# A threshold-attention and maxout-FFN kernel on one core: the same instructions in another written order, with other PSUM slots and another choice of masked score halves

## The chip, the cores and the metric

The kernel runs on one core of a Trainium2 chip. The core has a matrix engine (PE, called TensorE), a vector engine (DVE, VectorE), an activation engine (ACT, ScalarE), a general engine (POOL, GpSimd) and a queue that issues transfers (SP, SyncE). Each engine takes its own instructions in the order in which the program lists them, and semaphores hold an instruction back until what it needs is there. The metric is the device time of one execution in microseconds (us); smaller is better. Three runs of the kernel before took 442.86, 443.29 and 444.62 us, so the median is 443.29 us.

## The reference, cut to what matters

Eight batches of eight heads, 576 positions, head size 64. Scores that lie more than tau = 0.02 below their row's maximum are dropped, the rest go through a softmax. The result is the input of a feed-forward part with three first matrices, of whose products the elementwise maximum is taken.

```python
scores = scale * np.matmul(q, k.transpose(0, 1, 3, 2))
thresh = np.max(scores, axis=-1, keepdims=True) - tau
scores = np.where(scores >= thresh, scores, -1000000000.0)
scores = scores - np.max(scores, axis=-1, keepdims=True)
attn = np.exp(scores)
attn = attn / (np.sum(attn, axis=-1, keepdims=True) + 1e-09)
attn_out = np.matmul(attn, v)
...
x = attn_out.transpose(0, 2, 1, 3).reshape(B * S, H * D)
h = np.maximum(np.maximum(x @ w1, x @ w2), x @ w3)
out = h @ w_out
```

## The kernel before, in words

The attention is cut into 16 groups of four heads (a batch has two), and a group into nine chunks of 128 query rows and two halves each: 288 *score halves* of 128 x 576 in all. One letter of a long text, ORDER, issues one piece of work. The program at its end walks through this text, and every engine is wrapped so that its instructions stay in that order (class `_Ordered`). The letters that this document uses:

- `S` and a digit: the score matmuls of the next half, into one of four PSUM slots, the digit; a slot is two banks. `T` and a digit: transposes of queries and keys for a group (for the first group both into two slots, the digit's and the one two further on, with two small `warm` matmuls into slot 3 after the first of them). `O`: attention times values, `F` and `B`: the two halves of a feed-forward piece (tile `ph` for the hidden layer, `po` for the output), `N`: a piece of output rows.
- `m`: DVE reads a score half from PSUM, writes a copy `z` to SBUF and its row extreme `nm`. `s`: a tiny DVE instruction makes the threshold `th`. `e`: ACT makes exponents or clips at the threshold. `n`: ACT makes the exponents and their sum (an ACTIVATE and an ACTIVATION_READ_ACCUMULATOR). `k`: DVE drops what lies under the threshold and sums (SCALAR_TENSOR_TENSOR). `r`: DVE takes the reciprocal of the sums. `p`: POOL normalizes into `P`. `t`: SP issues the transposing transfer of `P` into `ptq`.
- `a`, `c`: ACT and DVE evacuate transposed queries `qt` and keys `kt`; `q`: POOL (for the first group DVE too) makes `qs`, a copy with the two 64-row halves swapped. `x`, `w`, `h`, `v`, `u`: evacuations of `O`, `F` and output pieces on ACT (`x`, `h`, `u`) and DVE (`w`, `v`).
- `l`, `g`: SP issues loads of inputs and of weights; `z`, `y`: POOL casts weights and values; `o`, `i`, `d`: stores.

A second text, MASKED, has a digit for each score half. It decides between two ways to the same numerators. For 0 and 2 (not masked) the half costs `m` on DVE and `e` and `n` on ACT; 0 also costs `s` on DVE. For 1 and 3 (masked) it costs `m` and `k` on DVE and `e` on ACT. With 2 and 3 (direct) `e` reads the scores from PSUM instead of `z`, and holds the slot until then.

Attention and feed-forward are interleaved: the first hidden-layer piece stands after the 54th score half, the last score half after some 140 of the 180 `F` pieces. The four PSUM slots are shared by all PE pieces, so a piece cannot start before the last reader of the piece that had its slot.

Of the kernel before, what the change touches and what calls it, by code (L numbers as in the profile page):

```python
# [21 lines left out]
FLAT = 2.0 ** -100  # L22

MASKED = """
320220312002220000101010000320210002020210010010301000000010100000001101
001001011010101100001000000000110000101010001111011000100000100010000000
110001001110100100010000001000111000000100011011101000011000010000010000
010101000111000100100000000101000000011110001110101000000000101000011121
"""


# [22 lines left out]
peBmF2pnvS0npS1rsmBnptmF3eT0ssvBatS1khF2qlemS0BerrpmT1epF3svtF0nsqcBeS2pvnBtpmeS1oyrS3mhpS2nmptF1nsmS0pleBrm
pF3nvS2teT0sslmF1eBkaBnsrqvS2hS0qmeF3ptmS1nBpsmnF2prevS0F1ptessmBpeBsvtF3hkS0lnBrmpleS1vT2peO0mnlscnT3lrwS1p
aF2mepS0treBpmF3nvyT1qnBcS0hpF2srempS1teS3mqBnkS0ptnO1smemteF3rvxlT0BskaS2evqS1npmS0tnysS3meF2smpermqeT0S1sc
pnBrmtepkyS0uS3muyS1epmS2lnF0pmoermpelS3skpO2elklnkO1elswnrmByxektpS1usrS3umS2peF0mpeS1mBynpsmtF3hS2srknpBtm
eS1F0pveF2sntmBnT3rvpS1atBpmeS0yrS3shmqtS1essF2mpeF0kqnF3smBetBrpvnlBprevS1lphS2lmnS0pmF3eptrS1mnBpmnF0ptsS2
veBosmeF1svT3nBtrecpS2hF0pmtnF3skBeT1srvS2paBtemqF0lnvS1pS2emBqermS3pnF1smT2eBchS3lskeT2O0lkakeqO2mtnsqlvS3x
wpS1nsrF2mpeF0rmpBestS3pevByemS1hS2tmpT3nF0rsmpnF1cBpeBtveT3S2rnvpS0astmpS1nmyS3eyF2smqnrstmepS1lnqS0mBelpsm  # L60
elkT1uS0ceS3lmeO1rknpiO0ewpumtnF1kelkxS2lkeS3sBrmepntpmF0uorS2rpuBnmyS3hsF1tmepT2lBkapS0essvS3eN2pmtnrmpF0ek
pS1jtBrnmF3lpnvS2opS1smeS0mBetS2mhS1ersmpF3tnF0kpBemF2sBrsevpBkF1qhtvS3nS2srpnrmBpeS0mF3pnmF2yteBvpeT0svqF1e
tBsscF3hkBnT2vS0aBemlqS2nvpF0nT1rmpBesS3cphF2rsmtpeS1rS0pnmS3teqBmF1epsvS0ntpsBmelT2ymO3evntrspF1welS0kaBnmS
3qS2hmpS0nrsF1mqeS3smpF2eBtrsmpnBvnpS0sS3epmS1etrvO0pelmekS2yxtmS3eF0mnpmnyT1yssrkS2npBemtpeclS3urS2pmuS1nsm
T0tO3akoeqO2elwpnlkT0eyrF3cximeqlS0snpBmeptskS1uF0mnBsurkpF1hrS2eBpmteS0pvF3lnS2prmeBpstF1mnF0peslvBkS2hS3rm
peBtrF1epsmT2npvBtaF3kpS0nsvBtemqS2ohS1rymnpF0sS3metpBemT2nF1rscpF3evBtqnBsvpS2hsrS0pemS1npmF2temT3S0assBnmF
3tnvS1S0ermpBemS2peF1svS0nmBerS3mpthS2kF0pnF1smeBrempO3nsvpteskF2qnBwBnrvtpT0eF3srscqS1hBepmT0S2vaS1smnqT3S0
mtnqF2secT1yBparmS3eqvS1eS0mpeF2mpempT3nS1ctqnS0smBermtnpS3kepS1muF0usrskpeS3meS2tpmeS1oBknmemnO3kuurO2kyxeO
1wetpsnkpS0xS2meF1rmnS3pBrsptmS0hF2pemS3perF1smBptnsS0vpeF3ktN2emeskBjF0rnvptBersS2pohBpF1evpF3nmBtnBkO0hsvt
eS2wrS1nrpmF3npsmS2eBpsmF1npvS0eytS2rsymBnpF3veipS0mBS1mhtF2nrsF3mpeBstpS1evF0emBeBvtS1hsF2nmS3nF0rsmpF1ekBp  # L70
nBvBesvO2hO3rkxpntS1rweS0pmF3nmpS2F1spremBpteBvpS0eS2vtS3mF1metkeF0mnnBrkpekBukurO1upoO2xpO1wprN3xptuF2jpF1h
F0tvF3vF1hF2vtF0vF1hF2vF0ovF1hF3vF2ivF1hF0vF2vF3hF0vO2vO3wF1xF0uF2hF3voF0vF2hF3vF1vF0hF2vF1vF0hF2vF1vF3hF2vF
0vF1hF2vF0vF2uF1ouN2ofjdi
"""


# [753 lines left out]
```

## Time and profile before

| what | value |
|---|---|
| median of three runs | 443.29 us (442.86 to 444.62) |
| the profiled execution | 443.79 us, of which the span from first to last instruction is 442.0 us |
| instructions | 14289 |
| busy: PE, DVE, ACT, POOL | 420.4, 398.2, 402.3, 319.5 us |
| weight loads of PE (PEld) | 318.1 us |
| mean granted TensorE clock | 0.987 of full speed |

The busy times are unions of an engine's instructions, so instructions that overlap in the engine's pipeline count once. The end of a matmul is modelled, and a busy PE is not one that works at its peak. A row that ends in `<-DVE z` tells that the engine stood idle before the instruction until DVE had written a tile `z`. Nearly all instructions carry line L93, that of the wrapper that keeps the order, so pieces are told apart by tile names.

### The profile page before, as it was taken

The numbers are of one execution on the slowest core, as the hardware profiler recorded it, in microseconds if no ns is written. First come the engines' busy times: TensorE is split into PE (matmuls) and PEld (weight loads), VectorE is DVE, ScalarE is ACT, GpSimd is POOL, SyncE is SP. The second block draws the span as 40 slices with busy tenths as digits, with TensorE's granted clock in tenths as the row PEclk, the third lists the DMA queues.
The fourth block names the chain that finished last, engine by engine and source line by source line (L and its number), as shares of the span: only waits on it lengthen the run. The fifth ranks groups of instructions, "written<-read, shape, count | busy, mean of one in ns | idle before, by whom it ended". The sixth has DMA issues, their size and how long they took to land.

```text
span 442.0 us, 14289 instructions
## 1 busy us (share of the span) xinstructions
PE 420.4 (95%) x5188; PEld 318.1 (72%) x5190; DVE 398.2 (90%) x1252; ACT 402.3 (91%) x828; POOL 319.5 (72%) x420
## 2 busy tenths in 40 slices
PE   8686879999999999999999999999999999999996
PEld 7453447787687777787788777787688786786873
DVE  3888899999999999999999998999999999899542
ACT  3999999999999999999999999999999999998421
POOL 1799999999889589866987676777777776555400
PEclk9998899999999999999999999999999999999999
DMA  6998999999999999999999999999999747987702
GB/s 190 280 294 175 258 197 240 274 222 270 232 241 250 222 204 228 220 200 236 200 227 224 215 173 244 209 200 198 178 252 197 124 82 129 185 132 110 188 25 85
DMA packets 213959, 88.50 MB, mean 200 GB/s; under 512 B 189184, under 2 KB 202240, under 8 KB 213888
## 3 DMA queue, kind: packets, MB, share of 16 engines
q1 hardware_dynamic: 213360, 86.96, 99.1%
q8 instruction: 41, 0.67, 0.6%
q10 hardware_dynamic: 528, 0.62, 0.5%
q14 instruction: 30, 0.25, 0.2%
HBM read 35.65 MB, written 9.44 MB: 102 GB/s over the span
## 4 chain that ended last, share of the span: by engine, by line
PE 84%; DVE 6%; ACT 5%; issue 2%; POOL 1%; DVEq 0%; POOLq 0%; ACTq 0%
PE ph L93 31%; PE sc L93 28%; PE po L93 10%; PE o L93 9%; ACT z L93 5%; DVE z L93 4%; PE tp L93 4%; PE warm L93 1%; POOL P L93 1%; DVE kt L93 1%; ACT qt L93 1%; DVE hm L93 0%; DVE stage L93 0%; DVE hT L93 0%; DVE th L93 0%
## 5 line engine op out<-in xcount | busy, mean ns | idle before, releaser
L93 POOL TENSOR_SCALAR P<-z,rs 128x576 bf16<-128x576 f32 x250 | 202.4, 821 | 61.5 <-DVE rs L93 23.3
L93 DVE TENSOR_SCALAR_CACHE_REDUCE z<-sc 128x576 f32<-128x576 f32 x250 | 184.1, 750 | 11.4 <-PE sc L93 5.2
L93 PE MATMUL sc<-kt,qs 64*128 64x256 f32 (+2 forms) x640 | 181.7, 419 | 8.2 <-DVE z L93 4.5
L93 PE MATMUL sc<-kt,qt 64*128 64x320 f32 (+2 forms) x640 | 182.2, 429 | 6.2 <-ACT z L93 2.7
L93 PE MATMUL ph<-xt,w 64*128 64x288 bf16 (+2 forms) x2160 | 171.3, 283 | 0.2
L93 PEld LDWEIGHTS <-w 64*128 64x128 bf16 (+1 forms) x2160 | 127.8, 94 | 32.2 <-issue 4.3
L93 ACT ACTIVATE z<-z,th 128x576 f32<-128x576 f32 x157 | 118.2, 770 | 1.7 <-DVE th L93 1.1
L93 ACT ACTIVATE z<-z 128x576 f32<-128x576 f32 x170 | 114.8, 678 | 0.3
L93 PEld LDWEIGHTS sc<-kt,qs 64*128 64x128 f32 (+1 forms) x640 | 93.4, 180 | 25.4 <-DVE z L93 9.5
L93 PEld LDWEIGHTS sc<-kt,qt 64*128 64x128 f32 (+1 forms) x640 | 93.2, 180 | 17.1 <-DVE z L93 5.2
L93 DVE SCALAR_TENSOR_TENSOR z<-z 128x576 f32<-128x576 f32 x80 | 67.2, 850 | 0.8 <-ACT z L93 0.8
L93 POOL COPY qs<-qt 64x640 f32<-64x640 f32 (+3 forms) x66 | 46.6, 705 | 23.0 <-ACT qt L93 19.7
L93 ACT ACTIVATE z<-z,nm 128x576 f32<-128x576 f32 x76 | 57.7, 767 | 1.1 <-DVE z L93 1.1
L93 PE MATMUL po<-wo,hT 64*128 64x512 bf16 (+3 forms) x454 | 53.1, 355 | 0.4 <-issue 0.2
L93 DVE TENSOR_TENSOR hm<-ph,hm 128x576 bf16<-128x576 f32 (+2 forms) x54 | 37.0, 685 | 10.9 <-PE ph L93 10.0
L93 ACT ACTIVATE hm<-ph 128x576 bf16<-128x576 f32 (+2 forms) x54 | 31.8, 589 | 13.0 <-PE ph L93 12.8
L93 PEld LDWEIGHTS <-hT 64*128 64x128 bf16 (+2 forms) x456 | 28.4, 95 | 18.7 <-issue 2.2
L93 DVE TENSOR_TENSOR hT<-ph,hm 128x576 bf16<-128x576 f32 (+2 forms) x54 | 37.0, 686 | 2.5 <-PE ph L93 0.7
L93 PE MATMUL o<-ptq,vb 128*64 128x512 bf16 (+2 forms) x544 | 38.7, 282 | 0.5 <-DVE z L93 0.5
L93 ACT ACTIVATION_READ_ACCUMULATOR z<-z 128x1 f32 x170 | 33.4, 196 | 0.0
L93 PEld LDWEIGHTS <-vb 128*64 128x64 bf16 x544 | 22.7, 111 | 13.9 <-issue 5.8
L93 POOL TENSOR_SCALAR P<-stage,rs 128x576 bf16<-128x576 f32 x38 | 29.5, 781 | 3.6 <-DVE rs L93 2.2
(44 smaller groups left out, 422.1 us busy)
## 6 DMA issues: line engine op xcount, KB each, us to landing
vm<-in_v_dram SPq DMA_DIRECT2D x32, 256.0 KB, 4.8
qm<-in_q_dram SPq DMA_DIRECT2D x15, 512.0 KB, 4.9
km<-in_k_dram SPq DMA_DIRECT2D x15, 512.0 KB, 5.6
out_dram<-ob SPq DMA_DIRECT2D x14, 512.0 KB, 3.9
stage<-in_moe_w_dram SPq DMA_DIRECT2D x9, 512.0 KB, 5.4
ptq<-P SPq DMA_TRANSPOSE x144, 4.5
vr<-in_v_dram SPq DMA_DIRECT2D x16, 128.0 KB, 3.7
stage<-in_moe_w_out_dram SPq DMA_DIRECT2D x3, 512.0 KB, 5.4
```

The lines of the kernel that those rows point to most:

```text
L93: ins = fn(*a, **kw)
```

## The change

Only the two tables change. The functions, the shapes, the pools and the numbers above them (36 warm matmuls, four slots, nine `z` buffers) stay.

```diff
 MASKED = """
-320220312002220000101010000320210002020210010010301000000010100000001101
+220202110002002100110000100020020312000112012010100000000010100000001100
...
 ORDER = """
-lllllllllT1lcaqqlT2S3agcqqmlS2S0elmlkeT1lmnS2lscS0aelrmS3plmeqmlqnS2zeslS1mT3nlpS0maygecreqekpS2nmnpT3meyskS
+lllllllllT0laqqlcT1aS2lcqqgmS0S3lemS1lmnT2lmeS3lsaS0mnqlqemT3lyerclcapsnS1lS2eqmlS3qemznmS2perS1mnpsmnpT3ske
...
```

Counted over the whole texts, the new MASKED has 187, 84, 14 and 3 of the digits 0, 1, 2 and 3, where the old one has 185, 86, 13 and 4. So 87 halves are masked instead of 90. ORDER keeps the kinds and numbers of all pieces apart from what follows from that: 201 `n` instead of 198, 87 `k` instead of 90, 187 `s` instead of 185. PE's large pieces keep nearly the same sequence; the digits of the slots, and the places of the short DVE, ACT, POOL and SP instructions between them, differ almost everywhere.

Counted in the written order, the ACT instructions ahead of the 60th score half are 114 in both (56 `e`, 41 `n`, 13 evacuations of transposes, 2 `x`, 2 `h`), ahead of the 72nd 138 in both, ahead of the 96th 190 before and 193 now, ahead of the 144th 293 and 295, ahead of the 216th 448 and 451.

Three places follow as rows of one engine's program. The first is DVE at the very start, where the first group's keys and queries come out of PSUM. Before:

```order
L93 MEMSET vr_102 64x64 x2
L93 COPY kt<-tp 128x320
L93 COPY qs<-qt 64x320
L93 COPY qs<-qt 64x256
L93 TENSOR_SCALAR z,nm<-sc 128x576 x2
L93 SCALAR_TENSOR_TENSOR z,sm<-z 128x576
```

and now:

```order
L93 MEMSET vr_102 64x64 x2
L93 COPY qs<-qt 64x320
L93 COPY kt<-tp 128x320
L93 COPY qs<-qt 64x256
L93 TENSOR_SCALAR z,nm<-sc 128x576 x4
L93 TENSOR_SCALAR th<-nm 128x1
```

The copy of the keys moves behind the copy of the swapped queries, and the first masked half's SCALAR_TENSOR_TENSOR is gone from here. At the same place the first transposes move from slot 1 (with 3) to slot 0 (with 2), and the second from slot 2 (with 0) to slot 1 (with 3). The two `warm` matmuls between them use slot 3 as before.

The second place is ACT over the same first microseconds, up to its first clipped half (`z<-z,th`). Before:

```order
L93 ACTIVATE qt<-tp 128x320
L93 ACTIVATE qt<-tp 128x256
L93 ACTIVATE kt<-tp 128x256
L93 ACTIVATE z<-sc,nm 128x576 x2
L93 ACTIVATE z,sm<-z 128x576
L93 ACTIVATE qt<-tp 128x320
L93 ACTIVATE z<-z,th 128x576
```

and now:

```order
L93 ACTIVATE qt<-tp 128x320
L93 ACTIVATE qt<-tp 128x256
L93 ACTIVATE kt<-tp 128x256
L93 ACTIVATE z<-sc,nm 128x576
L93 ACTIVATE z,sm<-z 128x576
L93 ACTIVATE z<-sc,nm 128x576
L93 ACTIVATE qt<-tp 128x320
L93 ACTIVATE z,sm<-z 128x576
L93 ACTIVATE z<-z,th 128x576
```

The first half is no longer masked, so its exponents and sum (`z,sm<-z`) follow on ACT at once, ahead of the second half's first instruction.

The third place is SP's queue around the loads of the third batch's first group (tiles `qm_870` and `km_872` before, `qm_901` and `km_903` now). Before:

```order
L93 DMA_TRANSPOSE ptq_736<-P_955 128x9x128
L93 DMA k8_873<-in_k_dram 128x4x64
L93 DMA stage_1036<-in_moe_w3_dram 128x4x256
L93 DMA qm_870<-in_q_dram 128x2x512
L93 DMA stage_1053<-in_moe_w1_dram 128x4x256
L93 DMA_TRANSPOSE ptq_1072<-P_999 128x9x128
L93 DMA km_872<-in_k_dram 128x2x512
```

and now:

```order
L93 DMA_TRANSPOSE ptq_749<-P_931 128x9x128
L93 DMA stage_1035<-in_moe_w3_dram 128x4x256
L93 DMA_TRANSPOSE ptq_1054<-P_1012 128x9x128
L93 DMA k8_904<-in_k_dram 128x4x64
L93 DMA qm_901<-in_q_dram 128x2x512
L93 DMA km_903<-in_k_dram 128x2x512
```

One transposing transfer of the next group now stands ahead of the load of the queries, and the load of the keys comes right behind it instead of two rows later.

More of the change, by code (lines that the diff above doesn't have):

```diff
@@ L24 @@
 MASKED = """
-320220312002220000101010000320210002020210010010301000000010100000001101
-001001011010101100001000000000110000101010001111011000100000100010000000
-110001001110100100010000001000111000000100011011101000011000010000010000
-010101000111000100100000000101000000011110001110101000000000101000011121
+220202110002002100110000100020020312000112012010100000000010100000001100
+001000111010000101100000000000110001100000011110110200100000100010000000
+110001101110100100010000001001100100000100101111102300000100100000001000
+001000110100100001000000000100100001011110100011011100002100001000001013
 """
@@ L71 @@
[L71 to L73 removed]
+lllllllllT0laqqlcT1aS2lcqqgmS0S3lemS1lmnT2lmeS3lsaS0mnqlqemT3lyerclcapsnS1lS2eqmlS3qemznmS2perS1mnpsmnpT3ske
+ytS1erkpT2agmnT3pclesqS2aqetS0meqlrnspmS1eqsT2nmpS3tnrcS0zlemS2eprmS3npmtS0npsgS1sermpS2emyS3eptmT0eplmS1ayl
+meS0kynS2tssT3snkynkercperlT3pmnpmntqremS0lasprgeT3pmeS2psstnplnS0mzecesqrmS3etqkeS2gpnmS1npsmtnS0prmleS3pmS
@@ new lines @@
+2npsmnS0yrsmetperS2epmO1eqtnkplemnzswT2teS3rplS1empnmS3tpnssrS1klepS0mapermtS2epmT1S3nmqtnkO2qemncpS3txrskT1
+peS2rmeS0ptmegpamS2npS1ertsmpnlkzS2elmS3eS0mpnlO1srkepsmnO2tyeprgwnpmT1xS3cpeS0sszmF2eS1meBqkF0ngqT3shrsmBay
+S2tvpnF3rpemS1BpemF0pnsvT2BnyctS1esrlsT2mphS3lezS1maF0myntpT2sS3ngrcqF1eBmpnS2svpBnrmS3peS0tmeyF2zmnF3lBsvep
+S0rhkBptesF2mgeS1zvF0nsmBpteBsrgvpnF1kS3phS2semBnqmF0S3evqF2ntrmBpelS1spvBnlmS3qhF0rsmepS1tnBpsmS3ezvS2eS1rm
+pF0etsyO3mnlkngpO2eswetkBxrmpT3nF2rvpaS1BnqmS0hspS3meF2prS1smntBzesmF3ezvT0tBeclT1yS2pnvS0apsmtS3eyrmlS1epS2
@@ new lines @@
+mepF0mnqsmnS3tkBnkeF1restpkumeS2prtBumlperkpS0ustS2umS3pesmS1eqtT0mO2nlpceqsrmO3ntywelkS0pxlS1meF3prnS2smBye
+myF0thpskS1oeBpF2nlvF3nlrmBpeBkpS1hstsvS0eF3lrmpnF2mBepBsveF1nT0vBtarkS3lhqS2smleF0prF1mnBysntBveS2plvnS0pom
+F3nyS1pmeBsysmF0thT2rrlpeS1clF3epsmBnqT2svBaS1evqS2nmF0pS3nmqBtnmT2pS1hrcpS3esmS0petF2melS1rmpBnF3skpetF0sve
+BlBmnF2vhtF1esrBkpnS0vtT3npBmS2arvpS0ermO3eqtsmepT1swntpS0cF2epesmtnS3kT1nS0mtBessrkpameS3preS1mS0uqmuS3mpnS
+1tsmS2pnoS0rempS3lempO1lnkqlemO2lnymeO0srkpetkeF3swxykxpT2BercnprtS1uyS2upmF0termqS3eBymN2lhsskpelkS0eF3ertm
@@ new lines @@
+S1pjBlmeS0plvF2npS1mnyF3tpmnBsopT0nvBaS1kF2ieqrssmS0hlpBmelT1qF3snrvF0epcBlepS2vBnpsmtS1nS3rmphS2mnpF1smeS0B
+snmF3tevS2T0mF1atBrsekpBevS0thS2pmF3nymS1qeBrsmnpS0tvF2eplF1rmnpBskeBptF3hsvS0eBrsstpmnS1lvT2qeO0mpnlscnT3wS
+1etF2srramS0lnqBmlF3eqvT1nBcpS0thF2pemS1perS3mpBnmS0ptesO1smpnkteF3yvxT0BraktyS2esS1vpeS0mpnS3meqF2mnyrmpnT0
+S1lceBqmeptrskS0pulS3muS1epmS2teF0rmplnskpeS1mtO3eklekO2esrmpesBknpwxS1kutS2urmopS3nF0myeS1mBetpsmF2hlS3rkep
+BlmnF0S1prnsvT3tepBmF2apsssvS1eBtqmeS0qrS3hmtS1epsmF2lnpF0mleF3koBnBrvpeBstyvS1phsS2nmF3emS0nrS1tpmBnprS2smn
@@ new lines @@
+F0pveF1pBsremT3ptevBpS2chF0tnmF3ekBT1nvS2aBsmlnF0qvS1eS2rtrespmS3eBmqF1hmpT2nBcpS3ekpT2O0sasvterlmpO2ekqntwS
+3xklpS1eF2ssmnF0yrBnmyS3evBptemS1plhS2ssmT3eyF0rcpeF1mBpntT3vnByS2ravpS0nmtpS3nsmS1eF2srmpektepS3slmnS0Bmeqn
+mT1ktuS3urS0lcpeO2rlmpelmpeO3klpelweF1kqnsxS0rkepS2tmS3eBymemepS0kuF3quT2smeBtrF1kphoS0aBmnpS3tsN2rnvplnmpS1
+erkpF0tjsF3mnBpsseBvS2ihrS1pmelS0mqeF3S2mnytBpmnoS1rF0eprsvF2ntpmBeBvqF1htskpS3esS0rmetS2pnmF3pBnmF0pesvT2te
+BcF1nsBrvpntBskphT2F3erS0vlapBmnF1qvS2etpBmT0hS3rscpnF2lmS1qesS0sempBemS3yF1nvtS0nmBnT2ssrmpO3etspveF0wnS1rk
@@ new lines @@
+BpaS3tmhS2elqsF1mlS0qnmS3ermpBF2espsmS0npvBeS3tmeS1rvpO0ntmnsmS2yxS3empF0eskyerT1mpeS2cBtnypsmelkS3ulS2muS1e
+smT0O3nsrplnpO2awetmeF3rkpxseT0S1ycntS2meF0poBrnsmpnkpF1ukBurS2shBqemF3oepvS0lS2nsmqF1emBptBnvF0hrrS2speS3mp
+F1emBpntT2vepF3BssaktS0nvlBemS2hS1rsmptF0nS3mpeBmtnT2F1svnF3cetBBsrnvpS2hsrqS0meS1pmeT3F2sprmaS0npBmeF3ptsvn
+S1qS0mnBtqmeS2yF1prevS0epssBmnS3qmS2htpmF0nlF1keBsmBertvO3pnvepF0serwpT2nBcpF3hktS1eBsrsmpnT0S2vtpaS1remqT3S
+0nmyF2qectT1BpasmS3epvS1nS0mqnF2rmpemtpT3eS1keqS0smBercntpS1mupS3emF0ukessS1rmtpnBmopkS2uskS1eO3rukekO0yxeO3
@@ L74 @@
+ynwtprmopS0xmpS2emF3peS1mteBrsmpS0nF2pmhtS1nkBS3evF0nstmN2erkpeF1mBjpsBevS2hskF0eF3rkpteBmF1nBpveBkO2hsrvpeS
+0rtwS1pnmF2npmS3eBympF1ntrvS0epBmpS2rF3svtpeS0mnpS1sBmiF2smhF0ntkBBervpS1etF3smpnF2BervpS1hsBpnmF0tevS3F1nmB
+etrBkpO2vhO3nspS1xrwepS0mpF3smS2etF1snmBeBstvnS2S0veS3meF1snkeF2rmpnmpeBnkBerrptukpuO3rN1xpuO0jpuO3wptF1xpF2
+hF0tvF1vF3hF0vtF1vF2hF0viF1vF2ohF0voF1vF3hF2vF1vF3hF2vO1vO0wF2xF3F1huF0vF3vF2ohF1vF3vF2hF0vF1vF3hF0vF2vF3hF1
+vF2vF0hF1vF2vF0uF1ouN0ofjdi
 """
```

29 lines of the change are left out of this document (removed).

## Prediction

> **What bounds the kernel now.** The page's first line has the busy time of each engine; three are close together.
>
> ```profile
> PE 420.4 (95%) x5188; PEld 318.1 (72%) x5190; DVE 398.2 (90%) x1252; ACT 402.3 (91%) x828; POOL 319.5 (72%) x420
> ```
>
> Which of them sets the pace differs by stretch, so the next view is the table of busy times by stretch. After the stretch and its length come the busy time of PE, PEld, DVE, ACT and POOL, with the number of instructions, then the granted TensorE clock.
>
> ```profile
> core 0: us, PE busy (x) PEld busy (x) DVE busy (x) ACT busy (x) POOL busy (x), PEclk, DMA share, GB/s
> 0.00:20.00 20.00, 14.53 (x132) 10.93 (x132) 11.67 (x38) 12.05 (x25) 8.53 (x18) 1.00 0.90 243
> 20.00:40.00 20.00, 15.97 (x138) 10.63 (x138) 17.47 (x57) 20.00 (x43) 19.05 (x27) 0.91 1.16 252
> 40.00:60.00 20.00, 14.80 (x114) 9.15 (x114) 17.67 (x60) 19.92 (x45) 19.17 (x25) 0.83 1.03 204
> 60.00:80.00 20.00, 18.07 (x226) 13.44 (x224) 19.67 (x66) 19.99 (x42) 18.20 (x23) 1.00 1.12 244
> 80.00:100.00 20.00, 19.99 (x264) 15.39 (x262) 19.54 (x63) 19.97 (x44) 19.12 (x27) 1.00 1.17 240
> 100.00:400.00 300.00, 299.29 (x3942) 231.85 (x3940) 289.79 (x919) 292.59 (x597) 225.66 (x294) 1.00 1.06 202
> 400.00:420.00 20.00, 20.00 (x239) 15.06 (x232) 14.41 (x40) 12.50 (x28) 9.79 (x12) 1.00 0.71 158
> 420.00:442.00 22.00, 17.73 (x152) 11.63 (x151) 7.93 (x16) 5.25 (x12) 0.00 (x0) 0.97 0.16 55
> ```
>
> There are two regimes. From 20 to 100 us ACT is busy for 79.88 of 80 us, while PE idles. From 100 to 400 us PE is busy for 299.29 of 300 us, and ACT has 7.41 us left over. So the time is a sum of four: until ACT runs without a gap, ACT's work up to the point where PE has enough queued to run without a gap, PE's remaining work, and the tail after PE's last matmul. The next view, PE's waits, agrees: first from 0 to 80 us, then all there are from 80 to 420 us.
>
> ```profile
> PE sc L93 <- DVE z L93: 6.6, 11, 1.2
> PE sc L93 <- ACT z L93: 3.7, 5, 1.3
> PE sc L93 <- DVE th L93: 1.5, 1, 1.5
> ...
> PE sc L93 <- DVE z L93: 0.2, 1, 0.2
> ```
>
> The scores wait for their slot's reader, but nearly all of it happens early, while ACT sets the pace. In the chain that ended last PE has most of the span:
>
> ```profile
> PE 84%; DVE 6%; ACT 5%; issue 2%; POOL 1%; DVEq 0%; POOLq 0%; ACTq 0%
> ```
>
> The profiled execution took 443.79 us, 1.8 us more than its span and 0.50 us over the median of 443.29 us. I work out a difference to the span and put it on the median.
>
> **The change part by part.**
>
> *Three halves go from masked to not masked.* Prices, from the costliest groups and the groups by line:
>
> ```profile
> L93 ACT ACTIVATE z<-z 128x576 f32<-128x576 f32 x170 | 114.8, 678 | 0.3
> L93 DVE SCALAR_TENSOR_TENSOR z<-z 128x576 f32<-128x576 f32 x80 | 67.2, 850 | 0.8 <-ACT z L93 0.8
> ...
> L93 ACT ACTIVATION_READ_ACCUMULATOR z<-z 128x1 f32 x170 | 33.4, 196 | 0.0
> L93 DVE TENSOR_SCALAR th<-nm 128x1 f32<-128x1 f32 x185 | 25.4, 144 | 0.5
> L93 DVE DVE_READ_ACCUMULATOR z<-z 128x1 f32 x80 | 6.3, 79 | 0.0
> ```
>
> ACT gets three more pairs of 678 + 196 ns, 2.6 us by durations. Neighbours overlap: in the next fence (the timeline of ACT's start, start and length in us) the pairs that begin at 18.38, 19.05 and 19.71 us are 0.67 us apart, so 2.0 us of ACT's time. DVE loses three of 850 + 79 ns and gets two `th` of 144 ns: 2.5 us less by durations. PE's work is the same. None of ACT's surplus stands in ACT's own regime: counted in the written order, ACT has 114 instructions ahead of the 60th score half and 138 ahead of the 72nd in both kernels, kind by kind equal, and the surplus begins between the 84th and the 96th. That is where PE takes over, and the 7.41 us of ACT's idle time cover it. So 0 on the path; if that cover is used up, up to 2.6 us. A gain from DVE's 2.5 us I take as 0 too, since PE hardly waits for DVE after 80 us (0.2 us above).
>
> *The start.*
>
> ```profile
> 5.89 0.44 ACT L93 ACTIVATE qt<-tp 128x320 f32<-128x320 f32 x1 [1.81 <-PE tp L93]
> 7.54 0.38 ACT L93 ACTIVATE qt<-tp 128x256 f32<-128x256 f32 x1 [1.21 <-PE tp L93]
> 7.82 0.38 ACT L93 ACTIVATE kt<-tp 128x256 f32<-128x256 f32 x1
> 9.53 0.74 ACT L93 ACTIVATE z<-sc,nm 128x576 f32<-128x576 f32 x1 [1.33 <-DVE z L93]
> 10.64 0.74 ACT L93 ACTIVATE z<-sc,nm 128x576 f32<-128x576 f32 x1 [0.38 <-DVE z L93]
> 12.59 0.44 ACT L93 ACTIVATE qt<-tp 128x320 f32<-128x320 f32 x1 [0.39 <-DVE kt L93]
> 12.92 0.77 ACT L93 ACTIVATE z<-z,th 128x576 f32<-128x576 f32 x1
> ...
> 18.38 0.69 ACT L93 ACTIVATE z<-z 128x576 f32<-128x576 f32 x1
> 19.05 0.69 ACT L93 ACTIVATE z<-z 128x576 f32<-128x576 f32 x1
> 19.71 0.74 ACT L93 ACTIVATE z<-sc,nm 128x576 f32<-128x576 f32 x1
> ```
>
> Beside it stand the matching rows of DVE and PE:
>
> ```profile
> 5.97 0.49 DVE L93 COPY kt<-tp 128x320 f32<-128x320 f32 x1 [4.30 <-PE tp L93]
> 6.49 0.61 DVE L93 COPY qs<-qt 64x320 f32<-64x320 f32 x1
> 6.51 0.37 PE L93 MATMUL warm<-vr 128*128 128x128 bf16 x2 [0.58 <-DVE kt L93]
> 7.30 0.74 PE L93 MATMUL sc<-kt,qs 64*128 64x256 f32 x1
> ```
>
> Before, the two warm matmuls wait 0.58 us for slot 3, because the first keys lie there; now these lie in slot 2, and that wait goes, so that the second transposes come some 0.6 us earlier. Late next is the copy of the keys: it now follows the copy of the swapped queries, which begins at 6.49 us as before (ACT's first copy ends at 5.89 + 0.44 = 6.33), so it ends at about 6.49 + 0.61 + 0.49 = 7.59 us instead of 6.46, and the first scores, which need it and its slot, begin at about 7.6 instead of 7.30 us. Behind this copy wait DVE's second `qs` copy and the first `m`; the first `m` and the first `e` come 0.3 us later, at 9.83. But then ACT no longer waits: the first half's second exponents follow at once and cover the 0.38 and 0.39 us gaps, in which ACT waited for the second `m` and for a key copy. Before, ACT had done seven instructions by 12.92 us. Now it has e, n, e, a, n by 9.83 + 4 x 0.67 + 0.44 = 12.95, with the three evacuations ahead eight. That is one instruction of 0.67 us more for 0.03 us: 0.6 us ahead, of which I keep 0.5, since the third transposes may still be late. Bounds: a gain of all three idle times after the first evacuations, 1.33 + 0.38 + 0.39 = 2.1, is excluded by the late first `m`, which leaves the two short ones, 0.8 us; a loss, if ACT keeps both gaps, is the 0.3 us of the late start. I take a gain of 0.5 us because the instructions that fill the gaps stand there by name. From then on ACT is gapless in both, so the gain travels on to 100 us and to the end.
>
> *ACT's work up to the crossing*: equal counts, 0. *PE's order after it*: the same pieces, and PE is dense; the 0.71 us that it idles from 100 to 400 us is the gain that is to be had, and as much again could be lost where a slot's digit now waits. I take 0, bounds -0.7 and +0.8.
>
> *SP's queue.* One transposing transfer moves ahead of the load of the third batch's first queries. Its SP rows, and the transposes on PE that need the load (all timelines), and the load's time to landing:
>
> ```profile
> 67.03 0.44 SPq L93 DMA_DIRECT2D qm<-in_q_dram  x1
> 68.08 2.81 SPq L93 DMA_TRANSPOSE ptq<-P  x1
> ...
> 75.19 0.45 PE L93 MATMUL tp<-identf,qm 64*128 64x64 f32 x7
> ...
> qm<-in_q_dram SPq DMA_DIRECT2D x15, 512.0 KB, 4.9
> ```
>
> A transpose holds SP for 2.81 us here. The load would be issued at 67.03 + 2.81 = 69.84 and land at 74.74, 0.45 us ahead of its use at 75.19. So 0, with little to spare; if the transfer before it waits longer for its `P`, the delay falls on PE directly, up to about 1 us. The other moves on SP, DVE and POOL lie behind ACT's 79.88 us, at 0. The thinnest of these covers is POOL's: from 40 to 60 us it is busy for 19.17 of 20 us, so an order on POOL that loses more than 0.83 us there would show.
>
> Sum: -0.5 + 0 + 0 + 0 = -0.5 us. That is 442.8 us on the median; a span of 441.5 us.
>
> **A rule weighed.** ACT idles from 100 to 400 us and PE does not; that row makes PE the bound there. The Trainium skill, Perfetto Trace Analysis, section Identifying the Most-Contended Engine, tells to judge vector and scalar engines by occupancy, and TensorE by its weight loads rather than by its matmul busy time. By it ACT (91%) would be the contended engine, ahead of the weight loads (72%), and ACT's 2.6 us would all count: the time would be that of the first rival, where the trace gives 442.8 us.
>
> **The rivals.**
>
> *ACT runs out of cover (slower).* Between 84 and 96 score halves three ACT instructions more are due, and ACT was full until 100 us. If PE there depends on ACT until later, the pairs come through at 0.67 to 0.87 us each. For it: ACT's row from 80 to 100 us, 19.97 of 20. Against it: PE's 19.99 in the same row. It decides if ACT's margin over PE behind the crossing is under 2 us. The time is 443.29 - 0.5 + 2.6 = 445.4 us, between 444.8 with 2.0 us and 446.2 with the start's loss of 0.3 in place of its gain.
>
> *The small waits shrink (faster).* From 60 to 80 us PE idles for 1.93 us, waiting for slots. If the new slots and the earlier start take these away, with the 0.5 us of the start the time is 443.29 - 0.5 - 1.9 = 440.9 us. For it: PE is nearly full at 80 us already. Against it: ACT is full in that stretch, so a wait that goes comes back at the next half.
>
> *The load is late (slower).* Its 0.45 us of margin turn into a wait of 1 to 3 us at 75 us: 443.8 to 445.8.
>
> *It does nothing*: the start's two effects cancel and the rest is noise of order: 443.3 us.
>
> **How the numbers follow.** A difference of 0.5%, 2.2 us, is about what a measurement tells from none. The forecast, 442.8 us, has 0.42; its own range is 441.8 to 444.4 us (the start 0.3 better or 0.8 worse, the order 0.7 better or 0.8 worse). Nothing done has 0.17. Both lie within 0.5%. ACT without cover has 0.18, half of it slower by over 0.5%, the small waits gone 0.15, nearly all of it faster by over 0.5%, the late load 0.08, half of it slower by over 0.5%. Of the forecast's own share I give 0.06 to faster and 0.05 to slower, for moves that no row prices. So faster 0.20, same 0.62, slower 0.18. The range of 8 in 10 takes in the faster rival and goes up to ACT's time, which leaves out half of that rival and the unpriced ends: 440.8 to 445.4 us.
>
> **What the profile after would show.** The start is right if ACT's first clipped half (`z<-z,th`) begins near 13 us with one more ACTIVATE ahead of it, and if the warm matmuls no longer wait for `kt`. ACT's cover is right if its idle time from 100 to 400 us falls from 7.4 to about 5 us and PE's stays under 1 us. The load is right if no transposes wait near 75 us. I am wrong if ACT has gaps between 20 and 100 us, or if PE's idle time after 100 us grows by over 2 us.

## The result, and the profile after

The kernel after takes 441.49 us in the median of seven runs (441.27 to 442.03), the kernel before 443.29 us in seven runs beside them. The ratio is 0.9957, with a 95% interval from 0.9943 to 0.9971, so 1.9 us less (1.3 to 2.5). Run again later beside other kernels, it gave 0.9961 (0.9940 to 0.9982). That is a gain, but one that lies within the 0.5% that the prediction took as the bound of what can be told.

The first part of the page, busy times, and its chain of work by engine:

```profile
PE 418.9 (95%) x5188; PEld 313.6 (71%) x5190; DVE 393.9 (89%) x1248; ACT 403.6 (92%) x834; POOL 317.0 (72%) x420
...
PE 78%; DVE 5%; POOL 5%; issue 4%; ACT 3%; DMA 2%; SPq 1%; DVEq 0%; POOLq 0%; ACTq 0%
```

ACT has six instructions more and DVE four fewer, as the three halves that are no longer masked make it. The chain now has 2% of DMA in it, which was not there before. The busy times by stretch, columns as in the prediction:

```profile
0.00:20.00 20.00, 14.54 (x150) 10.02 (x150) 12.69 (x44) 13.67 (x29) 10.43 (x21) 1.00 0.91 227
20.00:40.00 20.00, 14.38 (x120) 9.19 (x124) 16.92 (x59) 19.52 (x42) 17.20 (x24) 0.87 1.19 239
40.00:60.00 20.00, 16.06 (x126) 9.03 (x120) 17.54 (x61) 19.89 (x44) 19.47 (x25) 0.88 1.09 241
60.00:80.00 20.00, 18.14 (x226) 11.96 (x224) 18.52 (x63) 19.67 (x42) 18.76 (x25) 1.00 1.14 256
80.00:100.00 20.00, 20.00 (x266) 16.25 (x264) 19.45 (x63) 20.00 (x44) 18.99 (x26) 1.00 1.21 250
100.00:400.00 300.00, 299.60 (x3952) 231.38 (x3949) 288.27 (x913) 292.71 (x599) 225.80 (x297) 1.00 1.00 201
```

The two regimes are as before. ACT now idles for 0.92 us between 20 and 100 us (before 0.12), and PE for 0.40 us between 100 and 400 us (before 0.71). The waits of PE from 60 to 100 us show a load that was not waited for before:

```profile
PE sc L93 <- DVE z L93: 1.1, 2, 0.8
PE tp L93 <- DMA qm<-in_q_dram: 0.4, 1, 0.4
PE tp L93 <- DVE xt L93: 0.2, 1, 0.2
```

To see on which side of the crossing the time was won, I cut each profiled execution at one place that both programs share: the 101st matmul of the attention products (letter `O`), which begin with five of 20 matmuls each. In before it is the first of the sixth product. In after, where the end of the fifth and the start of the sixth overlap, it is the last of the fifth, 0.07 us behind the sixth's first. Ahead of the sixth product PE has issued the same other pieces in both: 75 score halves, 20 transposes, 15 `F` and 14 `B`. What comes before the cut I call the front, what follows to the end of the span the rest. PE's row of before and, in the next fence, that of after:

```profile
100.83 1.16 PE L93 MATMUL o<-ptq,vb 128*64 128x512 bf16 x16
```

```profile
100.18 0.19 PE L93 MATMUL o<-ptq,vr 128*64 128x64 bf16 x1
```

So before has a front of 100.83 us and a rest of 441.98 - 100.83 = 341.15 us; after has 100.18 and 440.23 - 100.18 = 340.05 us. By this one pair 0.65 us lie in the front and 1.1 us in the rest. The experiments ask which of the two is the change's.

### The profile page after: what moved, and what is told of

Read it like the earlier page. It is cut to its first block, busy times and chain, and to the rows that moved or that the text cites. A ratio compares the mean times of both kernels' runs of the same rounds, so it can differ in the third digit from the quotient of the medians.

```text
span 440.2 us, 14283 instructions
## 1 busy us (share of the span) xinstructions
PE 418.9 (95%) x5188; PEld 313.6 (71%) x5190; DVE 393.9 (89%) x1248; ACT 403.6 (92%) x834; POOL 317.0 (72%) x420
## 4 chain that ended last, share of the span: by engine, by line
PE 78%; DVE 5%; POOL 5%; issue 4%; ACT 3%; DMA 2%; SPq 1%; DVEq 0%; POOLq 0%; ACTq 0%
PE ph L93 31%; PE sc L93 26%; PE po L93 10%; PE o L93 8%; POOL P L93 4%; PE tp L93 3%; ACT z L93 3%; DVE z L93 3%; DMA qm<-in_q_dram 2%; SPq L93 1%; DVE kt L93 1%; POOL w L93 1%; DVE stage L93 0%; DVE hm L93 0%; POOL qs L93 0%
## 5 line engine op out<-in xcount | busy, mean ns | idle before, releaser
L93 PE MATMUL sc<-kt,qs 64*128 64x256 f32 (+2 forms) x640 | 179.8, 417 | 5.5 <-DVE z L93 3.9
L93 ACT ACTIVATE z<-z,th 128x576 f32<-128x576 f32 x161 | 120.5, 767 | 2.2 <-DVE th L93 1.9
L93 ACT ACTIVATE z<-z 128x576 f32<-128x576 f32 x175 | 117.6, 674 | 0.2
L93 PEld LDWEIGHTS sc<-kt,qs 64*128 64x128 f32 (+1 forms) x640 | 92.4, 179 | 22.5 <-DVE z L93 8.6
L93 PEld LDWEIGHTS sc<-kt,qt 64*128 64x128 f32 (+1 forms) x640 | 92.0, 179 | 14.7 <-DVE z L93 3.5
L93 DVE SCALAR_TENSOR_TENSOR z<-z 128x576 f32<-128x576 f32 x75 | 61.7, 827 | 1.4 <-ACT z L93 1.1
L93 ACT ACTIVATE z<-z,nm 128x576 f32<-128x576 f32 x72 | 53.9, 767 | 0.0
```

The costliest lines, as they stand in the source:

```text
L93: ins = fn(*a, **kw)
```

## The experiments

Single runs of a kernel scatter by 0.8 to 6 us here, so the ratios have intervals of 0.14 to 0.29% to each side. Fronts and rests come from one profiled execution each, which can be one of a kernel's faster or slower runs. The rests are finer all the same: those of kernels with the same order behind the sixth product agree within 0.5 us, but for one execution with a wait of its own (after, two loads earlier). The table has all of them, in us; the ratio is to the kernel before on the same chip.

| kernel | ratio (95% interval) | front | rest |
|---|---|---|---|
| before | | 100.83 | 341.15 |
| after | 0.9957 (0.9943 to 0.9971) | 100.18 | 340.05 |
| after, again | 0.9961 (0.9940 to 0.9982) | 101.48 | 340.22 |
| front of after, rest of before | 0.9991 (0.9964 to 1.0017) | 101.46 | 341.57 |
| front of before, rest of after | 0.9968 (0.9954 to 0.9983) | 101.12 | 339.88 |
| before, first 30 letters of after | 1.0001 (0.9985 to 1.0018) | 100.27 | 341.24 |
| the same, first half not masked | 0.9997 (0.9982 to 1.0013) | 100.81 | 341.60 |
| before, three halves not masked | 1.0011 (0.9990 to 1.0033) | 101.18 | 342.28 |
| after, three halves masked | 0.9995 (0.9970 to 1.0019) | 99.62 | 342.53 |
| before to 277 us, then after | 0.9993 (0.9964 to 1.0021) | 100.29 | 340.32 |
| after, three loads earlier | 1.0021 (0.9999 to 1.0044) | 101.38 | 340.08 |
| before, three others not masked | 1.0013 (0.9995 to 1.0031) | 99.86 | 341.49 |
| after, two loads earlier | 0.9969 (0.9947 to 0.9991) | 100.92 | 341.50 |
| before, with after's 277 to 354 us | 1.0002 (0.9979 to 1.0025) | 100.27 | 340.84 |

The expectations speak of the time "behind 100 us", 404.9 us for before: this is the span less what PE at 100 us is late against the sum of its pieces. For before it is some 64 us more than the rest in the table; only differences of it are used.

### Front of one, rest of the other

The two texts are cut just behind the sixth product and the transposes `T3` that follow it, where no slot changes its owner. The first pair of lines is the head of the text with the front of after, against before's. The second is its seam, against after's text; the third is the seam with the front of before, against before's text:

```diff
-lllllllllT1lcaqqlT2S3agcqqmlS2S0
+lllllllllT0laqqlcT1aS2lcqqgmS0S3
...
-gpO2eswetkBxrmpT3nF2rvpaS1BnqmS0
+gpO2eswetkBxrmpT3pvF1aS2rkepBtmnS3
...
-mO2esrwpeBgkpxT3vF1aS2rkepBtmnS3
+mO2esrwpeBgkpxT3snF2rvaS1BnqmS0
```

> The written order, the slots and the masks of the kernel after up to the 75th score half (about 102 us), those of the kernel before from there on (one threshold less and one normalization ahead at the seam). If the gain of 1.8 us was made at the start and carried to the end: 441.5 us. If it was made behind 100 us: 443.3 us. If the traces' own split holds (PE's distance to its cumulated work is 0.7 us shorter at 100 us and 1.1 us more is won behind): 442.6 us. If the start's gain in the trace of after was an accident of that execution: 443.3 us or up to 0.5 us above, for the late load and the first scores.

Measured: 0.9991, -0.4 us with an interval from -1.6 to +0.8, and a rest of 341.57 us.

> The reverse: the kernel before up to the 75th score half (about 102 us), the kernel after from there on. Gain made at the start: 443.3 us. Gain made behind 100 us: 441.5 us. The traces' own split: 442.2 us, with PE's idle time from 100 to 400 us near 0.4 us and the sum of small stalls between pieces about 1.1 us shorter than before.

Measured: 0.9968, -1.4 us (-2.0 to -0.8), and a rest of 339.88 us, like that of after. So the larger part of the gain sits behind the sixth product. The rests of the four kernels that have before's order there (before, front of after, and the two of the next section) are 341.15 to 341.60 us, mean 341.39. Those of the four that have after's unchanged (after twice, this one, and after with three loads earlier) are 339.88 to 340.22 us, mean 340.06: 1.33 us less. A fifth one, after with two loads earlier, has the same text there and a rest of 341.50 us, because of one wait of 1.12 us at 167.09 us; with it the difference of the means is 1.05 us. Measured behind that wait, the two sets of kernels do not overlap. PE's rows at the same transposes of queries near 200 us, in before and in after:

```profile
199.91 0.47 PE L93 MATMUL tp<-identf,qm 64*128 64x64 f32 x8
```

```profile
199.06 0.46 PE L93 MATMUL tp<-identf,qm 64*128 64x64 f32 x8
```

From there to the end of the span the four with before's order take 242.0 to 242.5 us (mean 242.2), all five with after's 241.2 to 241.3 us (mean 241.2): 1.0 us of the gain lie behind 200 us. What is left of it, between the cut and there, is below the scatter of that stretch, which can be over a microsecond. The granted clock is the full one from 54 to 439 us in all fourteen executions, so PE's speed is not what differs. The fronts show no such difference: 100.59 us in the mean of the six executions with before's front, 99.62 to 101.48 us in the four with after's, mean 100.69.

### The start alone

```diff
-lllllllllT1lcaqqlT2S3agcqqmlS2S0elmlkeT1lmnS2lscS0ae
+lllllllllT0laqqlcT1aS2lcqqgmS0S3lemlkeT1lmnS0lscS3ae
```

> The kernel before with the first 30 letters of the kernel after (the slots of the first transposes and scores, and the two key and query copies exchanged); the first half stays masked. Prediction's step: the warm matmuls' wait goes, the first scores come 0.3 us late, and nothing fills ACT's gaps: 443.6 us. Rival, slots are the gain: the second transposes come early and the first clipped half begins near 11.5 us: 442.2 us. In either case the profile shows whether TensorE's first transposes run at 0.22 us each (as after) or 0.31 us (as before) with the same 36 warm matmuls ahead; if 0.31 us appears here, the faster start of after is an accident of the execution and not of the change.

Measured: 1.0001. For the second kernel the first digit of MASKED becomes 2, and the `k` of the first half an `n`:

```diff
-320220312002220000
+220220312002220000
...
-lllllllllT1lcaqqlT2S3agcqqmlS2S0elmlkeT1lmnS2lscS0ae
+lllllllllT0laqqlcT1aS2lcqqgmS0S3lemnleT1lmnS0lscS3ae
```

> As the one with the first 30 letters of after, and the first score half not masked, its second exponents right behind the next first exponents as in after. Prediction's step: two ACT gaps of 0.38 and 0.39 us are filled, 442.8 us. If only slots count: the same as the one with the half masked. If the start is nothing: 443.3 us.

Measured: 0.9997. Neither can be told from no change, and a gain of 0.5 us could not have been. The profiles say more. With the first half still masked, ACT's first clipped half begins at 11.66 us with no instruction more ahead of it, and ACT waits 0.61 us for a key copy. An execution with before's start and PE at full speed from the same moment on, 4.4 us (before, with after's 277 to 354 us), has 11.66 us, too. So the slots alone gain nothing. With the first half not masked it is 11.94 us (full speed from 5.1 us on), with one ACTIVATE of 0.67 us more done: that is the gain.

### Does the early start of after come back?

The same kernel once more.

> The kernel after itself, once more, beside the others, for a second look at its start and at the load. If the first look's early start is the change's: the first clipped half begins near 11.5 us and TensorE's first transposes take 0.22 us each. If it was that execution's luck: near 12.0 us, with transposes of 0.31 us, and ACT's distance to its cumulated work at 20 us near 7.2 us instead of 6.7. The wait for the queries near 74 us lies between 0 and 1.4 us, as in the runs with the same front. Ratio to before as at first, 0.9957, if the gain is real.

Measured: 0.9961, and the start was not early. ACT's rows in this execution:

```profile
12.55 0.77 ACT L93 ACTIVATE z<-z,th 128x576 f32<-128x576 f32 x1
...
14.54 0.39 ACT L93 ACTIVATE qt<-tp 128x256 f32<-128x256 f32 x1 [0.60 <-DVE kt L93]
```

At first the clipped half began at 11.49 us in after and at 12.92 in before; now it begins at 12.55 us. What differs is PE's speed. PE's first score rows of after in the first execution and in this one (before had 0.74 and 0.86 us in the prediction's rows):

```profile
6.79 0.48 PE L93 MATMUL sc<-kt,qs 64*128 64x256 f32 x1 [0.36 <-DVE kt L93]
6.79 0.53 PE L93 MATMUL sc<-kt,qt 64*128 64x320 f32 x1
```

```profile
7.21 0.79 PE L93 MATMUL sc<-kt,qs 64*128 64x256 f32 x1 [0.33 <-DVE kt L93]
7.21 0.90 PE L93 MATMUL sc<-kt,qt 64*128 64x320 f32 x1
```

The same matmuls take 1.65 to 1.7 times as long. So the two executions of before and after that were compared first had different luck. The start is to be compared between executions at the same speed: before and this one, both slow, give 12.92 - 12.55 = 0.37 us, and one more ACTIVATE of 0.67 us done, less the 0.60 us for which ACT then waits: 0.4 us. Of those with an early full speed, the front of after has its clipped half at 11.71 and the front of before at 11.68 us (before to 277 us, then after), with the one ACTIVATE more and a wait of 0.25 us behind it: 0.03 us late, 0.67 - 0.25 - 0.03, again 0.4 us.

The gain cannot be found at the sixth product, and the load uses it up in part of the executions. PE's rows at the third batch's first queries, in after (first execution) and in the kernel with the front of after:

```profile
73.91 0.46 PE L93 MATMUL tp<-identf,qm 64*128 64x64 f32 x8 [0.42 <-DMA qm<-in_q_dram]
```

```profile
75.18 0.47 PE L93 MATMUL tp<-identf,qm 64*128 64x64 f32 x8 [1.43 <-DMA qm<-in_q_dram]
```

In the four executions with this front it waited 0.42, 1.43, 0.68 and 0 us (after, front of after, after again, after with three halves masked). Their fronts are 100.18, 101.46, 101.48 (the one with PE slow at the start) and 99.62 us. The wait reaches ACT, which sets the pace here: ACT waited 0.3, 1.5, 0.6 and 0 us for these transposes. ACT's waits from 20 to 104 us in the kernel with the front of after, of which the longer one, 1.5 us, is this:

```profile
ACT qt L93 <- PE tp L93: 1.8, 2, 1.5
```

That the load is all that hides the start's gain is not shown: the kernel with two loads earlier waits for none, and its front, 100.92 us, is no shorter than the mean.

### The masks alone

The kernel after has three masked halves fewer only behind the sixth product; ahead of it both kernels have as many. Behind it PE's late starts follow above all late reads by DVE (the section after this one shows one). So the first test takes masks off in before, in a stretch where six halves of twelve are masked.

```diff
-010101000111000100100000000101000000011110001110101000000000101000011121
+000001000101000100100000000101000000011110001110101000000000101000011121
...
-S3qS2hmpS0nrsF1mqeS3smpF2eBtrsmpnBvnpS0sS3epmS1etrvO0pelmekS2
+S3qS2hmspS0nrsF1mqeS3smspF2eBtrsmpnBvnpS0sS3enpmS1etrvO0penlmeS2
```

> The kernel before with three of its masked score halves (the 218th, 220th and 227th, whose pieces lie between 296 and 320 us) not masked: for each, DVE loses one multiply-and-sum and gets one threshold, ACT gets one more pair of second exponents. Nothing else moves. If the gain behind 102 us comes from DVE's lower load, which reads PE's slots sooner: about 0.8 us less than before, 442.6 us, and PE's small delays behind late slot readers on DVE from 296 to 330 us shrink from about 1.0 to 0.3 us. If it comes from the order and the slots: 443.4 us. If ACT lacks cover: 444 to 445.5 us.

Measured: 1.0011, and a rest of 342.28 us, 0.9 more than before's mean. DVE is relieved, but ACT is now full where these halves are. The busy times from 300 to 320 us of before, and, in the next two fences, those of this kernel and its PE's waits from 296 to 345 us:

```profile
300.00:320.00 20.00, 19.95 (x256) 14.21 (x253) 19.39 (x62) 19.69 (x41) 14.44 (x21) 1.00 1.04 186
```

```profile
300.00:320.00 20.00, 19.08 (x244) 13.92 (x241) 17.02 (x58) 20.00 (x45) 12.99 (x20) 1.00 0.99 182
```

```profile
PE po L93 <- ACT xt L93: 0.9, 1, 0.9
```

ACT had 0.31 us to spare here in before, and three pairs did not fit. The copy of a product behind them came late, and a piece of PE waited 0.9 us for it. Where the halves are, from 300 to 320 us, PE loses 0.65 us against before. The remaining loss, 0.5 us near 347 and 420 us, is one that the kernel with only the first half not masked has at the same places.

The reverse on the kernel after, the same three halves masked:

```diff
-001000110100100001000000000100100001011110100011011100002100001000001013
+011100110110100001000000000100100001011110100011011100002100001000001013
...
-S3tmhS2elqsF1mlS0qnmS3ermpBF2espsmS0npvBeS3tmeS1rvpO0ntmnsmS2
+S3tmhS2elqsF1mlS0qnmS3ermpBF2epmS0npvBeS3tmeS1rvpO0ntmksmS2
```

> The reverse on the kernel after: the same three halves masked, so that it has as many masked ones as the kernel before. If the masks carry the gain behind 102 us: 0.8 to 1.3 us more than after, 442.3 to 442.8 us. If order and slots carry it: 441.5 us.

Measured: 0.9995, 1.5 us more than after's 0.9961, and a rest of 342.53 us, 2.5 more than after's. Of these 2.5 us, 1.1 arise between 102 and 150 us, where its text is that of after, so they are not the masks' and show how far this stretch can scatter; 1.3 us arise between 300 and 345 us, where the three halves lie. Here DVE is late. PE's waits from 296 to 345 us:

```profile
PE sc L93 <- DVE z L93: 0.7, 2, 0.4
```

The third test takes masks off where ACT has a full microsecond to spare in 20:

```diff
-001001011010101100001000000000110000101010001111011000100000100010000000
-110001001110100100010000001000111000000100011011101000011000010000010000
+001001010010101000001000000000110000101010001111011000100000100010000000
+110001001110100100010000001000111000000100011011101000010000010000010000
...
-S0nsrzmS1etmS3peS2mpF0tskeqemF1nsrmpetBkpnkS3tuk
+S0nsrzmS1etmsS3peS2mpF0tskeqemF1nsrmpentBkpnkS3tu
```

> The kernel before with three other masked halves not masked: the 81st, 88th and 201st, with their pieces near 115, 129 and 286 us, in stretches in which ACT idles for a full microsecond in 20 (18.97, 18.98 and 18.99 us busy), whereas the three tried first lay where it has 0.3 to 0.6. Theory: what counts is whether ACT has room there; then PE's small delays behind DVE's late reads near 118, 120, 137 and 294 us (1.1 us together) shrink, and the stretch behind 100 us takes 0.4 to 1.0 us less than before's 404.9. Rival: any change of the masks without a new order costs, as the first three did (+0.9): 405.5 us or more behind 100 us.

Measured: 1.0013, and a rest of 341.49 us: nothing gained, 0.1 more than before's mean. The theory that room on ACT is all that counts fell. The 0.47 us by which before's PE was late at 118 us did go, but delays of 0.15 to 0.27 us came up at 126, 129 and 152 us, behind reads of ACT and DVE that now stand later in their order. So masks moved by themselves cost 0.1 to 1.3 us by these traces; none gained. What gained behind the sixth product is masks, written order and slots together. Which share the slots' digits have there was not tested: only those of the first 30 letters were tried alone.

### Where in the rest

```diff
-pS0essvS3eN2pmtnrmpF0ekpS1jtBrnmF3l
+pS0essvS3eN2pmtnrpnmpS1erkpF0tjsF3mn
```

> The kernel before up to the 200th score half (about 277 us), the kernel after from there on. By the traces, PE's distance to its cumulated work grows by 3.5 us from 300 to 400 us in before and by 2.5 in after, and by 6.1 and 6.0 us from 100 to 300 us: so two thirds or more of the 1.3 us lie here, 442.6 us. If the gain is spread evenly behind 102 us: 443.0 us. If it lies between 102 and 277 us: 443.5 us.

Measured: 0.9993 (-1.6 to +0.9 us) by the runs, which settles nothing, and a rest of 340.32 us, which is 1.1 us less than before's mean. The last test keeps only this stretch's first part and goes back to before's text at the 254th half:

```diff
-pS0essvS3eN2pmtnrmpF0ekpS1jtBrnmF3l
+pS0essvS3eN2pmtnrpnmpS1erkpF0tjsF3mn
...
-mpnT0S2vtpaS1remqT3S0nmyF2qectT1
+mpnT0S2vtpaS1resmnqT3S0mtnqF2se
```

> The kernel before with one stretch of the kernel after: order, slots and masks between the 200th and the 254th score half (about 277 to 354 us); all else as before. Theory: there the written order and the masks together let DVE read PE's slots in time, and PE's start-to-start delays from 277 to 345 us fall from 2.2 to 1.3 us: behind 100 us the span takes 404.0 us instead of before's 404.9, and the median falls by 0.9 us. Rival: the gain is spread over the whole stretch behind 100 us and hangs on the rest of the order: 404.6 us behind 100 us, a median 0.3 us under before's.

(The second pair of lines is after's text against this kernel's.) Measured: 1.0002 by the runs, and a rest of 340.84 us, 0.55 less than before's mean. Between 277 and 345 us PE gains most of what after gains there: its start-to-start delays, each piece's start against the usual distance between two such pieces, sum to 1.5 us, in after to 1.3 and in before to 2.2 us. From 345 to 400 us it loses 0.4 us of it (2.4 us of delays, against 2.0 in before). So the stretch is a place of the gain, but part of it needs the text behind it.

Such a delay does not show among the waits. This is the largest kind, PE's rows of before at a seam from key transposes to scores, and DVE's row that ends just ahead:

```profile
312.41 0.41 PE L93 MATMUL tp<-identf,km 64*128 64x64 f32 x8
312.65 0.23 PE L93 MATMUL tp<-identf,k 64*128 64x64 f32 x2
312.93 0.48 PE L93 MATMUL sc<-kt,qs 64*128 64x256 f32 x1
```

```profile
312.80 0.08 DVE L93 DVE_READ_ACCUMULATOR stage<-sc 128x1 f32 x1
```

PE's row has no wait behind it: the transposes' modelled end is 312.65 + 0.23 = 312.88, which is where DVE lets go of the slot. Matmuls overlap, though; in after the same pair of pieces starts 0.07 us apart instead of 0.28:

```profile
311.46 0.41 PE L93 MATMUL tp<-identf,km 64*128 64x64 f32 x8
311.70 0.23 PE L93 MATMUL tp<-identf,k 64*128 64x64 f32 x2
311.77 0.43 PE L93 MATMUL sc<-kt,qs 64*128 64x256 f32 x1
```

So 0.21 us are lost inside a stretch in which PE counts as 100% busy. The same can be counted over all of PE's starts from 277 to 345 us that come within 0.08 us of a semaphore, each against the distance that the quickest tenth of such pairs has, where it exceeds that by over 0.04 us (an estimate from the traces). The delays behind a semaphore of DVE sum to 1.4 us (11 starts) in before and in two others with its order, to 0.4 us (6 or 7) in after, in its second execution and in the kernel with its rest, and to 0.65 us (5) in the two kernels that take over after's text at 277 us. Those behind ACT's fall from 0.36 us to under 0.1. So fewer late readers, DVE's above all, are what PE gains there.

### The load, moved ahead

After waits for the third batch's queries, so two kernels issue that load earlier. First with all three loads ahead of a weight load (`g`) and a transposing transfer (`t`):

```diff
-S2rmeS0ptmegpamS2npS1ertsmpnlkzS2elmS3eS0mpnlO1s
+S2rmeS0ptmelllgpamS2npS1ertsmpnkzS2emS3eS0mpnO1s
```

> The kernel after with the three loads for the third batch's first group (the last keys, queries and keys) ahead of a weight load and a transposing transfer in SP's queue. The wait of 0.42 us for queries at 73.9 us goes. If it lies on the path: up to 0.4 us less than after, 441.1 us. If ACT sets the pace there and PE's wait is made up behind it: 441.5 us. If the later transposing transfers or weight loads are then late: 441.8 to 442.5 us.

Measured: 1.0021, by the two ratios some 2.7 us more than after's 0.9961. PE's wait for the queries went, and this came in its place (POOL's and DVE's waits from 60 to 104 us):

```profile
POOL w L93 <- DMA stage<-in_moe_w_dram: 2.3, 1, 2.3
```

```profile
DVE z L93 <- POOL P L93: 2.2, 2, 2.0
```

The weight load was issued 1.41 us later (66.34 instead of 64.93 us). POOL waited for it in its order, the normalizations queued behind came late, DVE could not reuse a `z`, and ACT waited 0.83 us for a threshold at 78.75 us. That this chain is worth the 2.7 us is not shown: the profiled execution is the fastest of its twelve runs (443.24 us, median 445.10), and its front and rest lie among those of after. Then with two loads ahead of the transposing transfer alone:

```diff
-S1ertsmpnlkzS2elmS3eS0mpnlO1s
+S1erlltsmpnkzS2emS3eS0mpnlO1s
```

> The kernel after with only two of the three loads (the last keys and the queries of the third batch's first group) ahead of the one transposing transfer, and the weight load left where it is. Theory from the trace with three loads moved: there the weight load came 1.4 us later, POOL waited 2.3 us for it, DVE 2.0 us for POOL, and ACT 0.8 us for DVE; so with the weight load in place neither that chain nor the wait for the queries appears, and ACT's distance to its cumulated work grows by under 0.4 us from 60 to 100 us: 441.2 to 441.5 us. Rival: the transposing transfer, 1.5 us later, is what POOL's results wait for: the same chain as before, 442 us or more.

Measured: 0.9969 (0.9947 to 0.9991). Neither the wait nor the chain appears, and PE waits between 60 and 100 us for slots alone (1.1 us for scores, 0.2 us for transposes). But the profiled execution has this wait for a transposed `P`, so its rest is 341.50 us:

```profile
167.09 1.12 PE L93 MATMUL o<-ptq,vb 128*64 128x512 bf16 x14 [1.12 <-DMA ptq<-P]
```

Whether the moved loads bring it about is not known. The runs do not show it faster than the kernel after; whether it equals it is open.

## Why the prediction was right, and where it was not

The prediction was 442.8 us, the measured time is 441.49 us; it lies in the range, and the change is within 0.5% as forecast. But the gain is not the one that the prediction counted. The start's gain cannot be found at the sixth product, and what shortens the kernel is a term that the prediction took as 0. That the forecast went the right way is in this sense luck.

*The start, -0.5 us.* Right in mechanism and nearly in size: the warm matmuls no longer wait for `kt`, one more ACTIVATE stands ahead of the first clipped half, and the gain is 0.4 us at equal speed of PE. The size owes something to two misses that cancel. The forecast had ACT's first exponents 0.3 us late, at 9.83 us; with PE slow they began at 9.48 us (9.53 in before), since the swapped copy began at 6.31 us instead of 6.49 and took 0.32 us instead of 0.61. And ACT then waited 0.60 us for a key copy, for which the forecast had kept back 0.1 us. The forecast moment, near 13 us, was 12.55 us with PE slow, and 11.5 to 12.0 us with PE fast. The working took the speed of before's execution as given, and that execution was a late one.

*The load, 0.* This is the term that failed beside the order. The prediction left 0.45 us of margin and gave the late load 0.08. It was late in three of the four executions with this front, by 0.4 to 1.4 us. In the first execution the issue came at 68.39 us, earlier than the 69.84 estimated, but the load took 5.48 us to land instead of the median 4.9, and its use would have come at 73.91 - 0.42 = 73.49 us, 1.7 us earlier than in before. The margin was taken from the use time of before, though a faster front moves the use forward. So the load can spend the start's 0.4 us; the fronts are alike in the mean. The prediction also said that it is wrong if ACT has gaps between 20 and 100 us. ACT has: 0.92 us in the first execution, of which 0.3 us follow from the load.

*PE's order after the crossing, 0, bounds -0.7 and +0.8.* This is the mis-sized term: it measured -1.0 to -1.3 us in the rests, outside its bound. The bound came from PE's idle time, 0.71 us, as "the gain that is to be had". But PE's delays there are mostly hidden in matmuls that overlap: start to start, waits for late readers of slots, above all DVE's, went down by more than PE's idle time has in all. The lines from 312.41 to 312.93 us show one. The rule that the prediction weighed (the Trainium skill, Perfetto Trace Analysis, section Identifying the Most-Contended Engine) says in its one half that matmul busy time is no good measure of how well TensorE is used, because matmuls are pipelined; that half is what the rests bear out, and the prediction read PE's idle time against it.

*Three halves not masked, ACT's cover, 0.* Right for the result: with 2.6 us more work on ACT the kernel is faster. By the other half of the same rule, which looks for the engine with the highest occupancy, ACT's extra work would have counted; neither comparison of the kernel after bears that out. The reason given was too coarse, however. The 7.41 us of idle time are no common stock: three pairs between 296 and 320 us, where ACT had 0.3 us to spare in 20, cost 0.65 us there. Nor was DVE's relief worth 0: three halves masked again cost after 1.3 us where they lie. The forecast that ACT's idle time falls to about 5 us was wrong, too. It is 7.29 us: the window from 100 to 400 us holds only two ACT instructions more than before (599 instead of 597), not six. PE's idle time stayed under 1 us, as forecast.

*The rivals.* "The small waits shrink" gave 440.9 us, nearer to the measured time than the forecast, from 1.9 us of waits between 60 and 80 us; a gain came, but elsewhere, behind 100 us, and by waits that the view of waits does not list. PE still idles for 1.86 us between 60 and 80 us. "ACT runs out of cover" exists as a mechanism, shown where halves were put without room, and does not act in after.

What is left open: of the gain of 1.3 to 2.5 us in the runs, 1.0 to 1.3 us are placed in the rest. Whether the front adds anything is below what fronts scatter (1.9 us). How the gain in the rest divides between order, slots and masks is open, too.

## What to carry to other kernels

A busy share of 100% for a pipelined engine is no bound on what its order can still gain: compare the starts of the same pair of pieces at several places, and look for a reader that ends just ahead of the late one. Idle time of a second engine covers new work only in the stretch in which it lies, and a choice between two engines (here the masks) goes with the order in which it was made. When a step makes something earlier, every load's margin is to be taken against the new use time; and a queue move is to be followed through each queue behind it, since the kernel with three loads moved ahead of one weight load lost more than the wait that was removed.

## What the runs showed of the hardware

PE starts at half its speed and changes to the full one at a time that the program does not fix. With the same 36 warm matmuls from 1.05 us on, 0.107 us apart at first and 0.056 us afterwards, the trace's record of the granted clock begins with this change, at 4.0 us in the first execution of after, between 4.4 and 6.6 us in eleven others, and at 10.5 us in before's and in the second execution of after. Until then the column PEclk shows 1.00 all the same, as in this row of before:

```profile
8.00:10.00 2.00, 2.00 (x11) 1.50 (x9) 1.16 (x4) 0.67 (x2) 0.50 (x1) 1.00 1.03 264
```

Between the two executions of after this is worth 12.55 - 11.49 = 1.06 us at the first clipped half. The Trainium skill (TensorE: Matmul & The Clock Gate, sections What you observe and What's actually happening) has the two spacings, which the trace agrees with, and puts the change near 4 us of sustained work, give or take 0.5 us, by windows of 3413 ns that run freely. Here it came 3 to 9.5 us after the first matmul.

Later the granted clock is halved for 3.41 us or a multiple (6.8, 10.2, 13.7), first from 12 to 24 us on and again from 36 to 43 us on, and both places and lengths differ between executions. One of the longest fell into the kernel with the front of before and the rest of after, whose mean from 40 to 60 us is 0.66 where before has 0.83, and ACT, which should be full there, is busy for 18.83 us:

```profile
40.00:60.00 20.00, 16.35 (x108) 10.62 (x110) 16.65 (x57) 18.83 (x41) 18.70 (x23) 0.66 1.05 213
```

The same load of 512 KB, the third batch's first queries, took 5.4 to 6.2 us from issue to landing in the four executions with after's front, at the same place of the program.
